# A token and channel mixer behind attention: the first channel product of the last two chunks in seven block products instead of eight

## The chip, the cores and the metric

The kernel runs on one core of a Trainium2 chip. The metric is the device time of one execution in microseconds (us). Five engines work side by side: TensorE (PE in the profile; PEld are its weight loads), VectorE (DVE), ScalarE (ACT), GpSimd (POOL) and SyncE (SP), which here issues the DMAs.

## The reference

Attention over 4 batches, 8 heads, 768 positions and head size 64, with a mask (8 global keys, a window of 96) and a linear bias; then a token mix and a channel mix, each of two products with a relu between. The mixes read the attention's output as `x` of 768 x 512 for each batch.

```python
def _moe_ref(x, w_tok1, w_tok2, w_ch1, w_ch2):
    xt = x.transpose(0, 2, 1)
    h = np.maximum(xt @ w_tok1, 0.0) @ w_tok2          # 768 -> 256 -> 768, over positions
    u = x + h.transpose(0, 2, 1)
    h2 = np.maximum(u @ w_ch1, 0.0) @ w_ch2            # 512 -> 1536 -> 512, over channels
    return (u + h2).astype(np.float32)
```

All is float32. The weights arrive as 64-bit words and are decoded on the chip.

## The kernel before

TensorE multiplies here in a float32 form that keeps fewer bits (F32R). Each operand is therefore split in a high part and a low part (`uh`, `ul` for u; `hh`, `hl` for the hidden layer; two halves of a `wc` tile for a channel weight), and each product is made of three matmuls: high by high, high by low, low by high. ScalarE makes the high part (copy or relu), VectorE or GpSimd subtracts it to get the low part.

The stages, all in one program:

- *Weights* (`weights`): 30 pieces of 128 x 512. ScalarE and VectorE decode them (two steps each), ScalarE makes the high part, VectorE or GpSimd the low. Pieces 0 to 5 are the token weights `w1h`, `w1l`, `w2h`, `w2l`; the rest the channel weights, `A[f]` (first product) and `Z[f]` (second), f from 0 to 11.
- *Attention* (`pair`): 48 steps, 12 to a batch, each of two heads and 256 queries: scores `sp`, maximum, exponent, sum, norm, transposes (by TensorE as `tp`, or from step 20 on by a DMA, `p<-r`), values `op`, and the output is put in `x`. Scores and values use TensorE in quarters of 64 x 64; everything else uses it whole.
- *Token mix* (`tokens`): per batch, six transposes `xtp`, first product `pj`, relu, and last product `pu` in tiles of 256 and 512 positions; VectorE adds `pu` to `x`, then `uh` and `ul` are made.
- *Channel mix* (`channel`): the 4 x 768 positions are cut into 6 chunks of 512 (`q`), so a chunk can span two batches. For each f, `first` makes a bank `hp` by 12 matmuls (4 slices of channels by 3), ScalarE takes its relu `hh`, VectorE the low part `hl`, and `second` adds 12 matmuls to four banks `acc` that are kept over all 12 f. At the end GpSimd makes `o` = uh + ul, VectorE adds `acc`, and SyncE stores it.

The order on every engine is written down ahead of time by `Plan.record`: each piece of work has a cost, a rank, what it must follow, and tokens that it takes and gives back (tile buffers by name, eight PSUM banks). The planner walks through its own clock and lets each engine take the ready piece of lowest rank; `TURN` is a price on changing between the two forms of TensorE. The ranks come from the tables at the end (`WEIGHTS`, `LOADS`, `CHANNEL`, `PAIRS`, `PRI`, `MIXES`). Each engine then runs its list strictly in order, so a wait holds up all that stands behind it. Because all operations pass through one helper, the profile shows line 235 for nearly all of them; the names of tiles tell them apart.

Of the kernel before, what the change touches and what calls it, by code (L numbers as in the profile page):

```python
# [9 lines left out]
F32 = mybir.dt.float32  # L10
# [58 lines left out]
def f32(ap):  # L69
    return ap.bitcast(F32)  # L70
# [173 lines left out]
class Fast:  # L244
# [157 lines left out]
    def pair(self, v):  # L402
# [132 lines left out]
        if v:  # L535
# [1 line left out]
                [f"load{v}"], r - PRI['q'])  # L537
        wp = ["w"] if wide else ["p", "p"]

        add(f"S{v}", "pe", 0.68 if j else 0.58, scores, ([f"q{v}"] if v else []) + ([f"ul{b - 1}{4 * len(spans(b - 1)) - 1}"] if b > 1 else []), r,  # L540
            [("sp", v, 0), ("sp", v, 1)], ["hl"] if FIRST <= v < PER else [], "quarters")
        for e in range(2):
            add(f"max{v}{e}", "dve", 0.58 if j else 0.52, lambda e=e: maxima(e), [f"S{v}"] + ([f"max{v}0"] if e else []),
# [27 lines left out]
    def tokens(self, b):  # L571
# [58 lines left out]

        def high_u(i):
            c, q, s, w, o = place(i)
            if o == 0:
                self.u[q, c] = [self.us.tile([P, W], F32R, tag=f"u{q % 2}", name=n) for n in ("uh", "ul")]
            act.copy(out=self.u[q, c][0][:, o:o + w], in_=self.x[b, c][:, s:s + w])

# [18 lines left out]
        for i in range(4 * len(segs)):  # L655
            c, q, s, w, o = place(i)
            k = r[NS + i]
            end = i // 4 == len(segs) - 1
            add(f"U{b}{i}", "pe", 6 * (w / 2400 + 0.013), lambda i=i: up(i),
                [f"jl{b}0", f"jl{b}1", "low3", "low4", "low5"] + ([f"U{b}{i - 1}"] if i else []), k, [("pu", b, i)],  # L660
                [tag] * 4 if i == 4 * len(segs) - 1 else [])
            add(f"ua{b}{i}", "dve", 0.12 + w / 900, lambda i=i: sum_(i), [f"U{b}{i}"], k - PRI['mix'], (), [("pu", b, i)])
            add(f"uh{b}{i}", "act", 0.1 + w / 1000, lambda i=i: high_u(i), [f"ua{b}{i}"], k - PRI['mix'], [f"u{q % 2}"] * 2 if o == 0 else [])
            add(f"ul{b}{i}", dict(pool=0.1 + w / 410, dve=0.12 + w / 900), 0, lambda en, i=i: low_u(i, en), [f"uh{b}{i}"],
                k - PRI['mix'], (), (["x"] if b else ["w"]) if end else [])


    def channel(self, q):

        add, dve, act, pool = self.plan.add, self.dve, self.act, self.pool  # L670
        last = CHUNKS * NF - 1
        hid, g = {}, {}

        def first(k):
            f = k % NF
            g["hp"] = ps = self.bank("hp", k)
            n = 0
            for c in range(4):
                for w, x in ((0, 0), (0, 1), (1, 0)):
                    self.pe.matmul(out=ps, lhsT=self.A[f][w][:, P * c:P * c + P], rhs=self.u[q, c][x],  # L680
                                   start=n == 0, stop=n == 11)
                    n += 1
            hid[k] = [ps, None, None]

        def high(k):
            hid[k][1:] = [self.hl.tile([P, W], F32R, tag="hl", name=n) for n in ("hh", "hl")]
            act.activation(out=hid[k][1], in_=hid[k][0], func=AF.Relu)

        def low(k):
            ps, hh, hl = hid[k]  # L690
# [11 lines left out]
        final = q == CHUNKS - 1  # L702

        def base(c):
            uh, ul = self.u[q, c]
            o = self.xs.tile([P, S], F32, tag="x", name="o")[:, :W] if final else self.io.tile([P, W], F32, tag="io", name="o")
# [12 lines left out]
        for f in range(NF):  # L719
            k = q * NF + f  # L720
            r = rank("channel", k)
            add(f"F{k}", "pe", 2.73, lambda k=k: first(k), ready + [f"low{6 + 2 * f}"] + ([f"F{k - 1}"] if k else []),
                r - PRI["F"], [("hp", k)])
            add(f"fh{k}", "act", 0.63, lambda k=k: high(k), [f"F{k}"], r - PRI['hid'], ["hl", "hl"])
            add(f"fl{k}", "dve", 0.7, lambda k=k: low(k), [f"fh{k}"], r - PRI["hid"], (), [("hp", k)])
            for i, cs in enumerate(((0,), (1,), (2,), (3,)) if k == last else ((0, 1), (2, 3))):
                add(f"G{k}{i}", "pe", 0.68 * len(cs), lambda k=k, cs=cs: second(k, cs),
                    [f"fl{k}", f"low{7 + 2 * f}"] + ([f"G{k}{i - 1}"] if i else [f"G{k - 1}1"] if k else []), r,
                    [("acc", q, c) for c in cs] if f == 0 else [], ["hl", "hl"] if cs[-1] == 3 else [])
        for c in range(4):  # L730
            add(f"base{q}{c}", "pool", 1.42, lambda c=c: base(c), [f"F{k}"], r, ["x" if final else "t"], [tag] * 2)
            add(f"out{q}{c}", "dve", 0.68, lambda c=c: total(c), [f"G{k}{c if k == last else c // 2}", f"base{q}{c}"], r - 30,
                [], [("acc", q, c)])
            pieces = parts(q)
            for i, cut in enumerate(pieces):
                add(f"store{q}{c}{i}", "sp", 0.7, lambda c=c, cut=cut: store(c, *cut), [f"out{q}{c}"], r - 30, (),
                    ["x" if final else "t"] if i == len(pieces) - 1 else [])

    def run(self):
        self.setup()  # L740
# [16 lines left out]

TURN = 96.75  # L760

BUSY = dict(dve=2.1, act=0.8, pool=1.6, sp=0.0)

# [284 lines left out]
```

## Time and profile before

| | us |
|---|---|
| median of 3 runs (lowest, highest) | 599.16 (597.72, 599.68) |
| the profiled execution | 596.46 |
| its span, first to last instruction | 595.1 |
| TensorE busy in it | 573.7 |
| VectorE, ScalarE, GpSimd busy | 307.4, 261.8, 208.5 |

The profile is of one execution. Its time is the span and 1.36 us around it. A busy time counts an engine as busy from an instruction's start to its end; matmuls overlap, so the distance from one start to the next tells more than the mean length of one. The granted TensorE clock was 0.997 of full speed over the span.

### The profile page before, as it was taken

Reading aid. Unit: us, or ns where it says so; the run is one execution under the profiler, and the core shown is the slowest. Engines: PE = TensorE matmul, PEld = TensorE weight load, DVE = VectorE, ACT = ScalarE, POOL = GpSimd, SP = SyncE. Lnnn points to the kernel's source line nnn. Section 1 sums busy time; section 2 is a strip of 40 time slices with the busy share of each in tenths; the row PEclk is TensorE's granted clock in tenths of the full one; section 3 lists DMA queues with packets and bytes.
Section 4 is the critical chain, followed back from the end, with each engine's and each line's share of the span. In section 5 each row is a group of like instructions: output and inputs, shape, how many; then the busy total and the mean of one; then the engine's idle time right before and its main releaser. Section 6 shows DMA issues by size and latency. Waiting matters only on the chain.

```text
span 595.1 us, 11893 instructions
## 1 busy us (share of the span) xinstructions
PE 573.7 (96%) x4456; PEld 465.4 (78%) x4456; DVE 307.4 (52%) x890; ACT 261.8 (44%) x713; POOL 208.5 (35%) x352
## 2 busy tenths in 40 slices
PE   4999999999999999999999999999999999999994
PEld 2878778778888878876888887677888888888883
DVE  5999999989433654574341147656526101121112
ACT  5999988987213443444330135646423101101010
POOL 4888787644212432443023026333504200040000
PEclk9999999999999999999999999999999999999998
DMA  7983378792001556386100015784201000020002
GB/s 266 342 350 117 116 253 306 198 257 91 0 2 70 140 133 150 77 169 160 50 1 1 0 72 116 183 172 127 54 1 66 6 0 1 0 72 0 1 0 77
DMA packets 62289, 62.46 MB, mean 105 GB/s; under 512 B 46864, under 2 KB 50064, under 8 KB 62224
## 3 DMA queue, kind: packets, MB, share of 16 engines
q1 hardware_dynamic: 62080, 61.62, 35.6%
q8 instruction: 37, 0.61, 0.4%
q14 instruction: 28, 0.23, 0.1%
q10 hardware_dynamic: 144, 0.00, 0.0%
HBM read 44.30 MB, written 6.29 MB: 85 GB/s over the span
## 4 chain that ended last, share of the span: by engine, by line
PE 82%; DMA 7%; DVE 4%; POOL 2%; issue 2%; SPq 1%; ACT 1%; POOLq 0%; DVEq 0%; ACTq 0%
PE acc L235 30%; PE hp L235 30%; PE pu L235 6%; PE pj L235 5%; PE op L235 5%; PE sp L235 4%; DMA e<-pk 3%; DMA p<-r 3%; PE tp L235 2%; PE xtp L235 1%; DVE pp L235 1%; DMA out<-o 1%; POOL pp L235 1%; POOL p L235 1%; DMA w<-wc 1%
## 5 line engine op out<-in xcount | busy, mean ns | idle before, releaser
L235 PE MATMUL hp<-uh,wc 128*128 128x512 f32 x576 | 185.3, 391 | 0.0
L235 PE MATMUL acc<-hh,wc 128*128 128x512 f32 x576 | 181.9, 397 | 0.0
L235 ACT ACTIVATE hh<-hp 128x512 fp32r<-128x512 f32 x72 | 42.9, 596 | 200.6 <-PE hp L235 198.6
L235 DVE SCALAR_TENSOR_TENSOR hl<-hp,hh 128x512 fp32r<-128x512 f32 x72 | 49.5, 687 | 155.1 <-ACT hh L235 155.0
L235 PEld LDWEIGHTS hp<-uh,wc 128*128 128x128 f32 x576 | 108.1, 188 | 23.4 <-issue 0.6
L235 PEld LDWEIGHTS acc<-hh,wc 128*128 128x128 f32 x576 | 105.2, 188 | 24.7 <-issue 3.3
L235 PE MATMUL acc<-hl,wc 128*128 128x512 f32 x288 | 112.7, 391 | 1.2 <-DVE hl L235 1.2
L235 PE MATMUL hp<-ul,wc 128*128 128x512 f32 x288 | 112.1, 389 | 0.0
L235 POOL TENSOR_SCALAR p<-p,st 128x192 f32<-128x192 f32 (+1 forms) x132 | 73.4, 574 | 34.1 <-DVE st L235 16.7
L235 DVE COPY r<-p 128x768 uint16<-128x768 uint16 x81 | 55.6, 694 | 43.7 <-POOL p L235 23.4
L235 PEld LDWEIGHTS acc<-hl,wc 128*128 128x128 f32 x288 | 54.1, 188 | 14.1 <-DVE hl L235 2.5
L235 PEld LDWEIGHTS hp<-ul,wc 128*128 128x128 f32 x288 | 54.1, 188 | 11.0
L235 ACT ACTIVATE p<-p,st 128x192 f32<-128x192 f32 (+1 forms) x132 | 57.4, 437 | 11.3 <-DVE st L235 11.1
L235 POOL TENSOR_TENSOR ul<-x,uh 128x512 fp32r<-128x512 f32 (+1 forms) x18 | 20.7, 1153 | 99.6 <-ACT uh L235 99.2
L235 POOL TENSOR_TENSOR o<-uh,ul 128x512 f32<-128x512 f32 x24 | 31.7, 1348 | 66.0 <-DMA out<-o 63.7
L235 POOL TENSOR_SCALAR e<-e,sc 128x256 f32<-128x256 f32 x37 | 21.6, 586 | 93.2 <-DMA e<-pk 82.8
L235 DVE SCALAR_TENSOR_TENSOR t<-w,t 128x512 int32<-128x512 int32 x60 | 47.2, 800 | 1.4 <-ACT w L235 0.9
L235 ACT COPY r<-p 128x768 uint16<-128x768 uint16 x31 | 32.9, 1067 | 32.8 <-DMA p<-r 30.9
L235 PE MATMUL sp<-e 64*64 64x192 f32 (+1 forms) x624 | 33.7, 332 | 10.1 <-ACT e L235 5.9
L235 DVE CUSTOM_DVE_ANT_0 p<-sp,bias 128x192 f32<-128x192 f32 (+1 forms) x132 | 37.7, 342 | 8.9 <-PE sp L235 8.8
L235 PEld LDWEIGHTS sp<-e 64*64 64x64 f32 x624 | 22.4, 139 | 15.7 <-ACT e L235 6.6
L235 PEld LDWEIGHTS op<-r,e 64*64 64x64 f32 x832 | 23.2, 133 | 10.5 <-issue 6.8
(90 smaller groups left out, 710.6 us busy)
## 6 DMA issues: line engine op xcount, KB each, us to landing
e<-pk SPq DMA_DIRECT2D x24, 592.0 KB, 4.0
w<-wc SPq DMA_DIRECT2D x24, 512.0 KB, 6.4
e<-pk SPq DMA_DIRECT2D x14, 560.0 KB, 5.3
out<-o SPq DMA_DIRECT2D x16, 256.0 KB, 2.1
unit<-pk SPq DMA_DIRECT2D x9, 384.0 KB, 5.4
w<-w SPq DMA_DIRECT2D x6, 512.0 KB, 7.4
out<-o SPq DMA_DIRECT2D x16, 128.0 KB, 1.9
keys<-pk SPq DMA_DIRECT2D x8, 208.0 KB, 5.2
```

What stands on the lines that cost most here:

```text
L235: ins = getattr(self.engine, name)(*args, **kw)
```

## The change

For the last two chunks (numbers 4 and 5) together, the first channel product is seen as a 2 x 2 block product: the channels in two halves, the pieces f and f + 6 as the two rows of weights, and the two chunks as the two columns of data. Strassen's scheme (in Winograd's form) needs seven block products for it where the plain one has eight. A *quad* is one f from 0 to 5; it gives four hidden tiles, called 11, 21 (chunk 4, pieces f and f + 6), 12, 22 (chunk 5).

- The data sums T1 to T4 are made once, behind the last batch's token mix: VectorE subtracts, ScalarE makes the high parts, VectorE the low parts (`td`, `th`, `tl`). They lie in the token weights' tiles and in attention buffers that are free by then.
- The weight sums S1, S2 are made for each quad a quad ahead, by GpSimd or VectorE (`sa`, `sb`), with high parts on ScalarE (`sh`) and low parts by VectorE or GpSimd (`sl`).
- The products `P` run in the order 1, 5, 2, 7, 6, 3, 4, six matmuls each, into four banks; 2, 3 and 4 add onto the bank of 1, 5 and 7.
- The sums of products are made by VectorE (`plus`), after a copy of product 1 by ScalarE (`keep`). Relu and low part follow as before, for chunk 5 into tiles that stay.
- The second product of chunk 4 (`G`) runs between the products; that of chunk 5 (`H`) comes last, one column of 128 channels after the other, 36 matmuls each. The last tile is added and stored in two halves.
- u of chunk 5 is split for two of its four channel slices only, and in the last batch by VectorE alone.
- The scores of batches 2 and 3 wait for the mix's last product instead of the last low part of u; and the planner's tables and `TURN` are new.

```diff
-        add(f"S{v}", "pe", 0.68 if j else 0.58, scores, ([f"q{v}"] if v else []) + ([f"ul{b - 1}{4 * len(spans(b - 1)) - 1}"] if b > 1 else []), r,
+        add(f"S{v}", "pe", 0.68 if j else 0.58, scores, ([f"q{v}"] if v else []) + ([f"U{b - 1}{4 * len(spans(b - 1)) - 1}"] if b > 1 else []), r,
...
+            if q == CHUNKS - 1 and c < 2:
+                continue
...
+        def product(f, x):
+            q = W // 2
+            a, b = self.A[f], self.A[f + M]
+            lhs = {1: [t[:, :q] for t in a], 2: [t[:, q:] for t in a], 4: [t[:, q:] for t in b]}
...
+            for d in range(2):
+                xs = {1: lambda: self.u[qa, d], 2: lambda: self.u[qa, d + 2], 3: lambda: self.u[qb, d + 2], 4: lambda: g["T", 4, d],
+                      5: lambda: g["T", 1, d], 6: lambda: g["T", 2, d], 7: lambda: g["T", 3, d]}[x]()
+                for w, r in ((0, 0), (0, 1), (1, 0)):
+                    pe.matmul(out=ps, lhsT=ws[w][:, P * d:P * d + P], rhs=xs[r], start=first and n == 0, stop=n == 5,
+                              skip_group_check=True)
+                    n += 1
+        def keep(f):
+            g["u2", f] = self.io.tile([P, W], F32, tag="io", name="u2")
+            act.copy(out=g["u2", f], in_=g["ps", f, 1])
+        def plus(f, out, ps, other):
+            if (out, f) not in g:
+                g[out, f] = self.mix.tile([P, W], F32, tag="p", name=out)
+            dve.tensor_tensor(out=g[out, f], in0=g["ps", f, ps], in1=g[other, f], op=ALU.add)
...
+        for f in range(M):
+            add(f"sa{f}", dict(dve=1.36, pool=2.84), 0, lambda e, f=f: whole(f, e),
+                [f"low{6 + 2 * f}", f"low{6 + 2 * (f + M)}", f"V{last_v - 1}"] + ([f"sb{f - 1}"] if f else []) + (["tl40", "tl41"] if f > 1 else []), s)
+            add(f"sb{f}", dict(dve=1.6, pool=3.2), 0, lambda e, f=f: mixed(f, e), [f"sa{f}", f"V{last_v}"] + ([f"sl{f - 1}0", f"sl{f - 1}1"] if f else []), s)
...
+            add(f"keep{f}", "act", 0.6, lambda f=f: keep(f), [f"P{f}1"], v, ["t"])
+            add(f"u2{f}", "dve", 0.68, lambda f=f: plus(f, "u2", 2, "u2"), [f"P{f}6", f"keep{f}"], v, (), [("hp", f, 2)])
+            add(f"u4{f}", "dve", 0.68, lambda f=f: plus(f, "u4", 3, "u2"), [f"P{f}5", f"u2{f}"], v, ["mix"])
+            add(f"u7{f}", "dve", 0.68, lambda f=f: plus(f, "u4", 4, "u4"), [f"P{f}7", f"u4{f}"], v)
+            add(f"c12{f}", "dve", 0.68, lambda f=f: plus(f, "c12", 3, "u2"), [f"P{f}3", f"u2{f}"], v, ["mix"], [("hp", f, 3)])
+            add(f"c21{f}", "dve", 0.68, lambda f=f: plus(f, "u2", 4, "u2"), [f"P{f}4", f"c12{f}"], v, (), [("hp", f, 4)])
...
+                if (q, c) == (qb, 3):
+                    b, s, w, o = pieces[0]
+                    pieces = [(b, s + i * w // 2, w // 2, o + i * w // 2) for i in range(2)]
...
-        for q in range(CHUNKS):
+        for q in range(CHUNKS - 2):
             self.channel(q)
+        self.last()
...
-TURN = 96.75
+TURN = 241.81
...
-PAIRS = [(103.53, 7.38), (232.79, 7.58), (299.85, 14.06)]
+PAIRS = [(119.72, 6.24), (217.78, 12.78), (353.61, 5.31)]
```

Three places of the planned order follow. On TensorE before, the end of a first product (`hp`) of chunks 4 and 5 and the start of the second product (`acc`) of the f before:

```order
L235 MATMUL hp<-uh,wc 128x512 x2
L235 MATMUL hp<-ul,wc 128x512
L235 MATMUL hp<-uh,wc 128x512
L235 MATMUL acc<-hh,wc 128x512 [waits Activation_49]
L235 MATMUL acc<-hh,wc 128x512
```

And with the change, products 1 (`uh`, `ul` by `wc`) and 5 (T1, which lies in `w2h` and `w2l`, by S1 in `w1h`) of a quad, ahead of the second product on the sum c21 of the quad before:

```order
L235 MATMUL hp<-uh,wc 128x512
L235 MATMUL hp<-ul,wc 128x512
L235 MATMUL hp<-uh,wc 128x512 x2
L235 MATMUL hp<-ul,wc 128x512
L235 MATMUL hp<-uh,wc 128x512
L235 MATMUL hp<-w2h,w1h 128x512 [waits Activation_49]
L235 MATMUL hp<-w2l,w1h 128x512
L235 MATMUL hp<-w2h,w1h 128x512
L235 MATMUL hp<-w2l,w1h 128x512 x3
L235 MATMUL acc<-hh,wc 128x512 [waits Activation_49]
L235 MATMUL acc<-hh,wc 128x512
L235 MATMUL acc<-hl,wc 128x512 [waits DVE_49]
```

Where 12 matmuls made one hidden tile, 12 make two products, and the second product behind them waits for ScalarE and VectorE's work on the product 4 that stands just ahead of these rows.

On VectorE before, the end of the program: the last batch's mix, then 12 low parts and 4 totals for each of the two chunks:

```order
L235 TENSOR_TENSOR x<-pu,x 128x512 x4
L235 TENSOR_TENSOR o<-acc,o 128x512 x4
L235 SCALAR_TENSOR_TENSOR hl<-hp,hh 128x512 x12
L235 TENSOR_TENSOR o<-acc,o 128x512 x4
```

With the change, one quad (`u_5641` is the running sum of product 1 and others, `u_5682` that for tile 22, `c_5709` is c12; `e_61` holds S1 and S2 in full):

```order
L235 SCALAR_TENSOR_TENSOR hl<-hp,hh 128x512 [waits Activation_49]
L235 TENSOR_TENSOR w1h<-e_61,w1h 128x512 [waits PE_49,Activation_49]
L235 TENSOR_TENSOR u_5641<-hp,u_5641 128x512 [waits DMAHW2_49,DVE_49,PE_49]
L235 TENSOR_TENSOR u_5682<-hp,u_5641 128x512 [waits DVE_49]
L235 TENSOR_TENSOR u_5682<-hp,u_5682 128x512 [waits DVE_49]
L235 SCALAR_TENSOR_TENSOR hid<-u_5682,hid 128x512 [waits DMAHW4_49,Activation_49]
L235 TENSOR_TENSOR c_5709<-hp,u_5641 128x512 [waits PE_49]
L235 TENSOR_TENSOR w1l<-e_61,w1h 128x512 [waits Activation_49]
L235 TENSOR_TENSOR u_5641<-hp,u_5641 128x512 [waits DVE_49,PE_49]
L235 SCALAR_TENSOR_TENSOR hid<-c_5709,hid 128x512 [waits Activation_49]
L235 SCALAR_TENSOR_TENSOR hl<-u_5641,hh 128x512 [waits Activation_49]
```

Two low parts for two f have become five sums, four low parts and two low parts of weight sums, and the low part of a weight sum (`w1l`) stands between c12 and c21.

On ScalarE before, behind the last batch's mix, the copies of u's high part and then nothing but relus:

```order
L235 ACTIVATE hh<-hp 128x512 [waits PE_49]
L235 CAST uh<-x 128x256 [waits DVE_49] x4
L235 CAST uh<-x 128x512 [waits DVE_49,Pool_49] x3
L235 CAST uh<-x 128x512 [waits Pool_49]
L235 ACTIVATE hh<-hp 128x512 [waits PE_49,Activation_49]
```

With the change, the same place ends in the first quad's copy of product 1 (`u_5641<-hp`):

```order
L235 ACTIVATE hh<-hp 128x512 [waits PE_49,Activation_49]
L235 CAST uh<-x 128x512 [waits Pool_49] x2
L235 CAST t_5615<-rough 128x512 [waits DVE_49,Pool_49]
L235 COPY u_5641<-hp 128x512 [waits DVE_49,DMAHW2_49,PE_49,Activation_49]
L235 ACTIVATE hh<-hp 128x512 [waits PE_49,Activation_49]
```

That copy waits for a DMA too (`DMAHW2`): the store of chunk 3's second tile, whose buffer it takes.

## Rows read from the trace of the kernel before

**Rows 1.** The page: busy time of each engine, share of the span, instructions.

```profile
PE 573.7 (96%) x4456; PEld 465.4 (78%) x4456; DVE 307.4 (52%) x890; ACT 261.8 (44%) x713; POOL 208.5 (35%) x352
```

**Rows 2.** Windows: length; busy TensorE, its loads, VectorE, ScalarE, GpSimd; clock; DMA; GB/s.

```profile
0.00:20.00 20.00, 11.64 (x138) 8.32 (x142) 12.45 (x71) 13.18 (x50) 9.60 (x44) 1.00 0.86 298
20.00:60.00 40.00, 38.76 (x680) 31.82 (x676) 39.02 (x159) 39.26 (x136) 34.47 (x75) 1.00 0.69 255
60.00:100.00 40.00, 38.16 (x409) 31.17 (x410) 37.21 (x97) 35.14 (x94) 30.00 (x36) 1.00 0.64 226
100.00:150.00 50.00, 49.96 (x377) 39.84 (x376) 44.04 (x92) 42.27 (x90) 27.02 (x30) 1.00 0.61 179
...
200.00:300.00 100.00, 98.50 (x868) 78.92 (x868) 53.34 (x165) 43.36 (x122) 31.45 (x60) 1.00 0.53 124
300.00:450.00 150.00, 149.26 (x1139) 120.59 (x1138) 72.48 (x219) 57.41 (x161) 45.94 (x77) 1.00 0.31 72
450.00:595.00 145.00, 137.44 (x607) 113.52 (x605) 27.70 (x41) 16.74 (x28) 16.50 (x13) 0.99 0.07 23
```

**Rows 3.** Chain of waits, last 200 us: start, length, engine and line, count.

```profile
413.90 1.59 PE acc L235 x6
...
431.31 1.38 PE acc L235 x6
...
445.83 8.34 PE pu L235 x48
...
576.57 5.44 PE hp L235 x24
582.01 3.41 PE acc L235 x15
```

**Rows 4.** Instructions by form, TensorE: operation, shapes, count | busy, mean ns | idle.

```profile
L235 PE MATMUL hp<-uh,wc 128*128 128x512 f32 x576 | 185.3, 391 | 0.0
...
L235 PEld LDWEIGHTS hp<-uh,wc 128*128 128x128 f32 x576 | 108.1, 188 | 23.4 <-issue 0.6 <-ACT x L235 0.3
```

**Rows 5.** Instructions by form, the other three engines (same columns).

```profile
L235 DVE SCALAR_TENSOR_TENSOR hl<-hp,hh 128x512 fp32r<-128x512 f32 x72 | 49.5, 687 | 155.1 <-ACT hh L235 155.0
L235 DVE SCALAR_TENSOR_TENSOR t<-w,t 128x512 int32<-128x512 int32 x60 | 47.2, 800 | 1.4 <-ACT w L235 0.9
L235 ACT ACTIVATE hh<-hp 128x512 fp32r<-128x512 f32 x72 | 42.9, 596 | 200.6 <-PE hp L235 198.6 <-PE acc L235 1.8
...
L235 POOL TENSOR_TENSOR wc<-t,wc 128x512 fp32r<-128x512 f32 x15 | 22.1, 1478 | 16.5 <-ACT wc L235 15.1 <-DMA w<-wc 1.3
...
L235 POOL TENSOR_TENSOR ul<-x,uh 128x512 fp32r<-128x512 f32 x12 | 15.6, 1300 | 59.1 <-ACT uh L235 58.7
...
L235 DVE TENSOR_TENSOR x<-pu,x 128x512 f32<-128x512 f32 x16 | 11.0, 690 | 6.9 <-PE pu L235 6.7
...
L235 DVE TENSOR_TENSOR wc<-t,wc 128x512 fp32r<-128x512 f32 x9 | 6.8, 759 | 1.1 <-ACT wc L235 1.1
L235 DVE TENSOR_TENSOR x<-pu,x 128x256 f32<-128x256 f32 x16 | 6.4, 419 | 5.4 <-PE pu L235 5.1
...
L235 POOL TENSOR_TENSOR ul<-x,uh 128x256 fp32r<-128x256 f32 x6 | 5.1, 860 | 40.5 <-ACT uh L235 40.5
```

**Rows 6.** Timeline of the end: start, length, engine, operation, idle before it.

```profile
585.51 2.73 DVE L235 TENSOR_TENSOR o<-acc,o 128x512 f32<-128x512 f32 x4 [2.15 <-PE acc L235]
...
586.23 3.61 SPq L235 DMA_DIRECT2D out<-o  x4
...
587.06 0.39 PE L235 MATMUL acc<-hl,wc 128*128 128x512 f32 x1
```

**Rows 7.** DMA issues on the page; the output tile; the closing semaphores.

```profile
out<-o SPq DMA_DIRECT2D x16, 128.0 KB, 1.9
...
DMA to landing us min/median/max: 1.7/2.0/6.7
...
L1044 SPq EVENT_SEMAPHORE  x8: 17/28/28, 592.8 to 595.1; - x8
```

More of the change, by code (lines that the diff above doesn't have):

```diff
@@ L632, in high_u @@
             c, q, s, w, o = place(i)
-            if o == 0:
+            if (q, c) not in self.u:
                 self.u[q, c] = [self.us.tile([P, W], F32R, tag=f"u{q % 2}", name=n) for n in ("uh", "ul")]
@@ L662, in tokens @@
             add(f"ua{b}{i}", "dve", 0.12 + w / 900, lambda i=i: sum_(i), [f"U{b}{i}"], k - PRI['mix'], (), [("pu", b, i)])
+            if q == CHUNKS - 1 and c < 2:
+                continue
             add(f"uh{b}{i}", "act", 0.1 + w / 1000, lambda i=i: high_u(i), [f"ua{b}{i}"], k - PRI['mix'], [f"u{q % 2}"] * 2 if o == 0 else [])
-            add(f"ul{b}{i}", dict(pool=0.1 + w / 410, dve=0.12 + w / 900), 0, lambda en, i=i: low_u(i, en), [f"uh{b}{i}"],
-                k - PRI['mix'], (), (["x"] if b else ["w"]) if end else [])
+            add(f"ul{b}{i}", dict(dve=0.12 + w / 900) if b == B - 1 else dict(pool=0.1 + w / 410, dve=0.12 + w / 900), 0, lambda en, i=i: low_u(i, en), [f"uh{b}{i}"],
+                k - PRI['mix'], (), ([] if b == B - 1 else ["x"] if b else ["w"]) if end else [])
     def channel(self, q):
         add, dve, act, pool = self.plan.add, self.dve, self.act, self.pool
-        last = CHUNKS * NF - 1
         hid, g = {}, {}
@@ L700, in second @@
                                    start=f == 0 and i == 0, stop=f == NF - 1 and i == 2)
-        final = q == CHUNKS - 1
         def base(c):
             uh, ul = self.u[q, c]
-            o = self.xs.tile([P, S], F32, tag="x", name="o")[:, :W] if final else self.io.tile([P, W], F32, tag="io", name="o")
+            o = self.io.tile([P, W], F32, tag="io", name="o")
             g["o", c] = o
@@ L723, in channel @@
                 r - PRI["F"], [("hp", k)])
[L724 to L728, printed above, removed]
+            add(f"fh_{k}", "act", 0.63, lambda k=k: high(k), [f"F{k}"], r - PRI['hid'], ["hl", "hl"])
+            add(f"fl_{k}", "dve", 0.7, lambda k=k: low(k), [f"fh_{k}"], r - PRI["hid"], (), [("hp", k)])
+            for i, cs in enumerate(((0, 1), (2, 3))):
+                add(f"g{k}_{i}", "pe", 0.68 * len(cs), lambda k=k, cs=cs: second(k, cs),
+                    [f"fl_{k}", f"low{7 + 2 * f}"] + ([f"g{k}_{i - 1}"] if i else [f"g{k - 1}_1"] if k else []), r,
                     [("acc", q, c) for c in cs] if f == 0 else [], ["hl", "hl"] if cs[-1] == 3 else [])
         for c in range(4):
-            add(f"base{q}{c}", "pool", 1.42, lambda c=c: base(c), [f"F{k}"], r, ["x" if final else "t"], [tag] * 2)
-            add(f"out{q}{c}", "dve", 0.68, lambda c=c: total(c), [f"G{k}{c if k == last else c // 2}", f"base{q}{c}"], r - 30,
+            add(f"base{q}{c}", "pool", 1.42, lambda c=c: base(c), [f"F{k}"], r, ["t"], [tag] * 2)
+            add(f"out{q}{c}", "dve", 0.68, lambda c=c: total(c), [f"g{k}_{c // 2}", f"base{q}{c}"], r - 30,
                 [], [("acc", q, c)])
@@ L788, in rank @@
         return CHANNEL[0] + CHANNEL[1] * at[0]
-WEIGHTS = [71.26, 9.54, 24.38, 24.05]
-LOADS = [13.15, 6.65, 38.51, 3.54]
-CHANNEL = [162.7, 6.43]
-PAIRS = [(103.53, 7.38), (232.79, 7.58), (299.85, 14.06)]
-PRI = {'q': -1.3, 'max': 19.6, 'exp': 3.4, 'sum': 46.9, 'norm': -2.6, 'T': -2.6, 'back': 11.2, 'split': -78.6, 'join': -1.1, 'V': 47.2, 'put': 16.0, 'F': 5.5, 'mix': 1.2, 'hid': 28.8, 'high': 15.9}
-MIXES = [-31.47, 214.66, 304.69]
+WEIGHTS = [82.59, 11.43, 0.91, 26.98]
+LOADS = [10.58, 4.16, 407.44, 1.08]
+CHANNEL = [176.2, 6.52]
+PAIRS = [(119.72, 6.24), (217.78, 12.78), (353.61, 5.31)]
+PRI = {'q': -16.6, 'max': 27.3, 'exp': -7.0, 'sum': 90.7, 'norm': -19.4, 'T': -22.4, 'back': 52.4, 'split': -95.1, 'join': 5.2, 'V': 13.2, 'put': 25.2, 'F': 7.0, 'mix': -9.7, 'hid': 49.7, 'high': 21.0}
+PRI2 = {'early': 159.0, 'quad': 34.3, 'mixed': 108.7, 'second': -69.0, 'step': -14.4, 'tail': -66.4}
+MIXES = [154.62, 92.38, 36.73]
 @with_exitstack
```

175 lines of the change are left out of this document (174 added, 1 removed).

## The prediction

> **What bounds the kernel now.** I read the engines' busy times first, then the same by stage, then the chain of waits of the last 200 us, then single operations and the tail. TensorE is busy 573.7 of 595.1 us, every other engine half of it or less [rows 1]. By stage, TensorE lacks 8.36 us in the first 20, then 1.24, 1.84, 0.04, 1.50 and 0.74 in the stages shown from 20 to 450 us, 5.36 together; VectorE and ScalarE are as full as TensorE only up to 100 us (39.02 and 39.26 of 40 us between 20 and 60). From 450 us on it lacks 7.56 us, all behind the last matmul, which starts at 587.06 and runs 0.39 [rows 2, 6]. In the chain the end is nothing but first and second products back to back: 24 matmuls in 5.44 us, so 226.7 ns each [rows 3]. Their weight loads take 188 ns, less than that, and stay beneath them [rows 4]. So a 128x512 matmul taken out between 150 us and the end is worth 226.7 ns, as long as its successors never wait.
>
> **The change, part by part.**
>
> *Products removed.* Two chunks with 12 pieces each of 12 matmuls are 288 for the first product. Now six quads of seven products of six matmuls do it: 252. The order of TensorE agrees, 36 rows fewer, all else equal in count. 36 x 0.2267 = -8.16 us. I found no row of a product accumulated over six matmuls in a bank of its own with sums over several banks behind it, but the mix's last product is six matmuls to a bank: 48 of them, half 256 wide, take 8.34 us without a gap [rows 3]. So a six-matmul group pays no entry price: 0 extra; the other end is the price of a change of form, 0.21 us for each of 42 products, 8.8 us.
>
> *Sums added, VectorE and ScalarE.* A quad adds on VectorE five sums of PSUM (0.69 each, as the mix's sum), four lows (0.69) and two lows of the weight sums (0.76): 7.7 us; on ScalarE a copy, four relus and two copies, 7 x 0.60 = 4.2 us [rows 5]. A quad is 42 + 24 = 66 matmuls, 14.96 us, and lies in a stage in which both engines are nearly idle (27.70 and 16.74 us of 145) [rows 2]. Totals fit twice over, so only chains can cost. The tightest is the second product of the sum c21. Count from the end E of product 4: product 3 ended at E-1.36; VectorE makes c12, then the weight low queued behind it (until E+0.19), then c21 (E+0.88), low 12 (E+1.57), low 21, whose relu was ready at E+1.58 (E+2.36). TensorE has products 1 and 5 of the next quad first (12 matmuls, 2.72 us) and two matmuls on the high part, so it asks at E+3.17: 0.8 us to spare. Product 5 needs the bank that c12 empties, at E-0.57, and asks at E+1.36. The low behind product 2 (0.60 + 0.69 + 0.1) is hidden by products 7 and 6 (2.72). Cost 0. If all cover were gone: 1.4 + 2.4 us, some 3.8 per quad, 23 us.
>
> *The sums before the first quad.* After the mix's last product TensorE has 66 matmuls of the chunks before (14.96 us; the kernel before has 12). VectorE then has 19 instructions up to the last low of the sums T, 19 x 0.69 = 13.1 us [rows 5], and of these only the first six stand before product 5, which comes at 16.3 us. Cost 0. One wait is new in kind: ScalarE's copy of product 1 takes a buffer that the second store of chunk 3 must have left. Its last product ends at 13.6 us, two totals 0.69 each make 15.1, the store lands 2.0 us later [rows 7], the copy needs 0.60: 17.8, and product 2, which must not write before, would start at 17.7. With the relu behind it in ScalarE's queue I put +0.3 us; with landings of 1.7 and 6.7 us [rows 7] it is 0 and +4.8. The DMA is quiet there (share 0.07) [rows 2], so the median counts.
>
> *Weight sums on GpSimd.* Two of 512 (1.30) and four of 256 (0.86) per quad: 6.0 of 14.96 us [rows 5], a quad ahead: 0 by themselves. But a rule speaks against them. The low of a channel weight, with both inputs in SBUF, took VectorE 0.759 us; the low of the hidden layer, with one in PSUM, 0.687; GpSimd's weight lows took 1.478 where its token lows took 1.300 [rows 5]. So a meeting costs VectorE under 0.1 us on the mean: three such lows in the tight chain give 0.2 of the 0.8 us to spare, and nothing in the sum. The Trainium skill (SBUF — State Buffer, section Who interferes with whom) says that a VectorE instruction with two SBUF inputs contends with a GpSimd one that reads SBUF, and that the loser fully blocks for the whole instruction; the trace shows lengthening, not whole blocks. That mechanism is the slower rival below.
>
> *The tail.* Before: four totals, one behind each quarter of the last product, four stores of 256 KB crowded together; the fourth is issued at about 588.3 and SyncE sees it landed at 592.8 [rows 6, 7], 5.35 us after the last matmul's end at 587.45. Now the four columns are finished one after another, 36 matmuls (8.16 us) apart, so only the last tile is late, in two halves: two totals of 256 (0.42 each, 0.1 to start) [rows 5], then a 128 KB store, 1.9 us [rows 7]: 2.9 us. -2.45 us; ends 0 (the last store as slow as now) and -2.6.
>
> *The attention's order.* The scores' wait now ends with the mix's last product, the price of a form change rises to 241.81 and all ranks are new. In TensorE's order the runs of one form fall by four, two returns from quarter form to full: six matmuls after such a return take 1.59 us, elsewhere 1.38 [rows 3], so about 0.23 each way with the entry, -0.5 us together. For the waits, the first and second products that stand between a batch's first scores and its transposes rise from 192 to 252 (batch 1), 330 to 432 (batch 2), 228 to 258 (batch 3): each wait has more behind it. At best all 5.36 us of idle go; at worst as much comes on top (an estimate: no row bounds it). I take -1.0.
>
> Sum: -8.16 - 2.45 - 0.5 - 1.0 + 0.3 = -11.8. The profiled execution took 596.46, span 595.1 plus 1.36: it would take 584.7. The median of the runs shown is 2.7 us above it; the same step from 599.16 gives 587.4.
>
> **Rivals.**
> 1. *The order costs instead of paying.* For: batch 1's mix now comes after 2.5 more weight pairs, five pieces of two 0.80 us steps each, 8.0 us of VectorE [rows 5] in a stage where it has 8.75 of 90 us free [rows 2]. Against: the 60 extra products give TensorE 13.6 us of work meanwhile. Idle doubles: 587.4 + 1.0 + 5.4 = 593.8.
> 2. *GpSimd holds VectorE up, and it gets slower.* Place: in each quad the next weight sums on GpSimd start right when the weight low is done, beside c21, low 12 and low 21. If each of three two-input lows waited for a whole GpSimd sum of 1.30, that is 3.9, less 0.8 to spare, 3.1 us on six quads: 18.6, giving 606. It decides from a hold-up of 0.8 + 11.8/6 = 2.8 us per quad. Against: 0.759 beside 0.687. A mild form, one block of 1.30 in each quad, costs 0.5 x 6 = 3 us: 590.4.
> 3. *The change doesn't do what it says:* 42 short products pay 0.21 us each to enter, and 8.8 of the gain is lost: 596.2. Against: the gapless 48 of the mix.
>
> **How the numbers follow.** Forecast 0.66 (its own range 584 to 590); rival 1 0.14; the mild form of 2 0.09; 2 in full 0.05; 3 0.06. About 0.3%, 1.8 us, is what a measurement of this kernel can tell from no change, so faster means under 597.4. The first three cases are faster, 0.89; rival 3 mostly too, half of it within the bound: faster 0.92, same 0.03, slower 0.05. Low end: idle halves (-2.7 for -1.0), no new wait, a shorter tail still: 583. High end: rival 1, 593.8. Left out are most of 2 in full and of 3, and a little below.
>
> **What would show it.** 5.44 us per 24 matmuls in the last 130 us without idle before acc or hp, and matmuls of the two chunks' first product at 252: step 1. The time from the last matmul's end to SyncE's first closing semaphore near 2.9 us: the tail. TensorE's idle between 20 and 450 us under 5.4: the order. A gap before the first quad's second product shows the buffer. Wrong it is if TensorE waits on VectorE in every quad, or if VectorE's two-input lows grow beyond 0.9 us.

## The result and the profile after

| | before | after |
|---|---|---|
| median of the compared runs, us | 598.60 (597.72 to 599.68, 4 runs) | 591.41 (590.07 to 593.89, 4 runs) |
| ratio, 95% interval | | 0.9884 [0.9842, 0.9926] |
| profiled execution, us | 596.46 | 593.89 |
| its span | 595.1 | 592.0 |
| last matmul's end | 587.45 | 585.14 |

The change saves 7.2 us by the medians, where 11.8 were forecast. The two profiled executions are only 2.6 us apart: that of before lies 2.1 us under its median, that of after 2.5 above its own. What the traces show must therefore be split by stage and compared over more than one execution.

The page's first part, as in [rows 1]: TensorE has 36 matmuls and 6.7 us of work less, VectorE 49.5 us more.

```profile
PE 567.0 (96%) x4420; PEld 460.4 (78%) x4420; DVE 356.9 (60%) x952; ACT 276.2 (47%) x743; POOL 234.4 (40%) x377
```

Windows of after, for [rows 2] (same columns; the last one begins 3 us behind the mix's end):

```profile
20.00:60.00 40.00, 36.69 (x649) 30.53 (x642) 38.67 (x156) 37.88 (x133) 35.19 (x75) 1.00 0.65 241
...
100.00:150.00 50.00, 47.45 (x321) 37.36 (x320) 44.97 (x85) 40.92 (x84) 30.04 (x29) 0.97 0.62 183
...
200.00:300.00 100.00, 100.00 (x793) 81.12 (x792) 49.93 (x153) 36.54 (x107) 28.89 (x52) 1.00 0.48 113
300.00:450.00 150.00, 148.47 (x1197) 119.50 (x1196) 84.22 (x231) 64.80 (x180) 57.80 (x91) 1.00 0.36 80
450.00:592.00 142.00, 134.91 (x594) 111.01 (x592) 66.08 (x95) 29.59 (x49) 26.39 (x25) 0.99 0.07 23
```

TensorE lacks 3.31 us between 20 and 60 (1.24 before) and 2.55 between 100 and 150 (0.04 before, and there at a granted clock of 0.97); between 200 and 300 it lacks nothing more (1.50 before). From 20 to 450 us it lacks 9.3 us in all, where the forecast wanted under 5.4. So the order moved idle time to the front, where the forecast had it shrink.

The largest new wait, in the timeline of after (start, length, engine, operation; in brackets the idle time before and what ended it):

```profile
127.75 5.17 DVE L235 SCALAR_TENSOR_TENSOR t<-w,t 128x512 int32<-128x512 int32 x5 [0.51 <-issue]
...
131.50 1.19 PE L235 MATMUL sp<-e 64*64 64x192 f32 x18
...
134.05 0.68 DVE L235 SCALAR_TENSOR_TENSOR hl<-hp,hh 128x512 fp32r<-128x512 f32 x1
...
134.78 1.55 PE L235 MATMUL sp<-e 64*64 64x192 f32 x14 [2.10 <-DVE hl L235]
```

Scores wait 2.1 us for the bank that a low part of the hidden layer empties. That low part stands on VectorE behind five steps of weight decoding and more; the waits of before show none between 100 and 150 us. Behind the wait the granted clock is near the lower of its two levels for 3.3 us (columns as in [rows 2]):

```profile
134.70:138.00 3.30, 3.22 (x19) 2.19 (x20) 3.27 (x10) 2.29 (x6) 1.87 (x2) 0.53 0.00 0
```

So the wait costs more than its 2.1 us, by some 1.5 us (an estimate: 3.3 us at about half speed).

The chain of waits at the end, for [rows 3]:

```profile
450.83 1.70 DVE rough L235
...
453.74 1.71 DVE w1l L235
...
455.47 1.29 DVE rough L235 x2
456.76 0.61 DVE hl L235
...
457.42 5.28 PE acc L235 x22
462.70 6.84 PE hp L235 x30
469.54 2.72 PE acc L235 x12
472.26 5.44 PE hp L235 x24
...
549.78 35.37 PE acc L235 x156
...
585.18 0.08 DVE x L235
```

From 457.4 on it is products back to back: 24 first products in 5.44 us, as in [rows 3], and 156 second products in 35.37, 226.7 ns each. Ahead of that, VectorE's queue of sums is the chain, up to a low part that waits for its turn there and that a second product of the cover needs; two of the steps (a sum and a low part) have 1.70 and 1.71 us in it, where their neighbours have 0.6. The timeline of after shows what they met there, and the same for low 21 in a quad:

```profile
450.31 1.68 POOL L235 TENSOR_TENSOR o<-uh,ul 128x512 f32<-128x512 f32 x1 [6.95 <-DVE t L235]
450.75 1.78 DVE L235 TENSOR_TENSOR rough<-x,rough 128x512 f32<-128x512 f32 x1
...
490.05 1.89 POOL L235 TENSOR_TENSOR e<-e,e 128x256 f32<-128x256 f32 x2 [4.12 <-DVE w1l L235]
491.37 1.12 DVE L235 SCALAR_TENSOR_TENSOR hl<-u,hh 128x512 fp32r<-128x512 f32 x1
```

GpSimd ends at 451.99 and 491.94, VectorE 0.54 and 0.55 us later, at 452.53 and 492.49: here a VectorE instruction of 0.69 with two inputs in SBUF hardly moves until GpSimd's has ended.

### The profile page after: what moved, and what is told of

Same layout as the page of the kernel before. It is cut to its first block, busy times and chain, and to the rows that moved or that the text cites. A ratio compares the mean times of both kernels' runs of the same rounds, so it can differ in the third digit from the quotient of the medians.

```text
span 592.0 us, 11933 instructions
## 1 busy us (share of the span) xinstructions
PE 567.0 (96%) x4420; PEld 460.4 (78%) x4420; DVE 356.9 (60%) x952; ACT 276.2 (47%) x743; POOL 234.4 (40%) x377
## 5 line engine op out<-in xcount | busy, mean ns | idle before, releaser
L235 PE MATMUL acc<-hh,wc 128*128 128x512 f32 x480 | 152.1, 398 | 0.0
L235 PE MATMUL hp<-uh,wc 128*128 128x512 f32 x432 | 144.8, 394 | 0.0
L235 PEld LDWEIGHTS acc<-hh,wc 128*128 128x128 f32 x480 | 88.2, 189 | 21.2 <-issue 2.8
L235 PEld LDWEIGHTS hp<-uh,wc 128*128 128x128 f32 x432 | 81.1, 188 | 18.4 <-ACT x L235 0.6
L235 PE MATMUL acc<-hl,wc 128*128 128x512 f32 x240 | 94.3, 393 | 0.2 <-DVE hl L235 0.2
L235 PE MATMUL hp<-ul,wc 128*128 128x512 f32 x216 | 84.3, 390 | 0.0
L235 ACT ACTIVATE hh<-hp 128x512 fp32r<-128x512 f32 x54 | 32.1, 594 | 83.8 <-PE hp L235 82.0
L235 DVE SCALAR_TENSOR_TENSOR hl<-hp,hh 128x512 fp32r<-128x512 f32 x54 | 36.9, 683 | 52.2 <-ACT hh L235 52.0
L235 PEld LDWEIGHTS hp<-ul,wc 128*128 128x128 f32 x216 | 40.6, 188 | 7.9
L235 PE MATMUL acc<-hid,wc 128*128 128x512 f32 x144 | 33.0, 389 | 0.0
## 6 DMA issues: line engine op xcount, KB each, us to landing
e<-pk SPq DMA_DIRECT2D x24, 592.0 KB, 4.3
```

Of the source, the lines that this page charges most:

```text
L235: ins = getattr(self.engine, name)(*args, **kw)
```

## How the stages are compared

Orders put different numbers of first and second products into a stage. To compare it, take its length by the end of a batch's last mix product (`pu`; the start of the next matmul is taken for it), and subtract 0.2267 us for each first and second product that stands in it. What is left is attention, mixes and waits:

| run | to batch 1's mix | on to batch 2's | on to batch 3's | sum |
|---|---|---|---|---|
| before | 109.8 | 43.0 | 42.5 | 195.3 |
| after | 117.3 | 38.5 | 44.8 | 200.6 |

For before, batch 1's mix ends at 164.4 behind 241 products (the one that starts then counted in): 164.4 - 54.6 = 109.8; for after at 180.1 behind 277. The profiled executions of e1, e4 and e5 have after's order of the attention; their sums are 201.0, 197.1 and 200.4, so one execution is good for 2 us or so, and the mean of the four is 199.8. Part of that scatter goes with the clock: between 100 and 150 us it is 0.97 in after, e1, e3 and e6, which take 116.7 to 118.8 us to batch 1's mix, and 1.00 in e4 and e5, which take 115.3 and 115.6; the order up to there is the same in all six.

## Experiments

Ratios are to the kernel before on the same chip, with 95% intervals.

**e1: eight products.** Product 1 runs twice, so the first product has its 288 matmuls again.

```diff
-            for d in range(2):
+            for d in ((0, 1, 0, 1) if x == 1 else (0, 1)):
...
-                    pe.matmul(out=ps, ..., start=first and n == 0, stop=n == 5, ...)
+                    pe.matmul(out=ps, ..., start=first and n % 6 == 0, stop=n % 6 == 5, ...)
```

> The changed kernel with the six matmuls of product 1 made twice in each quad, the first time overwritten: 36 matmuls of 128x512 more, nothing else. Theory 1 (TensorE is the bound of the last stage and of the whole): each costs its 226.7 ns, 36 x 0.2267 = 8.16 us more than the changed kernel, 599.6 against 591.4, and the last matmul ends 8.2 us later. Theory 2 (the quads wait for VectorE's sums, so part of the removed matmuls were idle time anyway): less than 6 us more, since the longer product 1 hides waits.

Measured: 600.22 us, 1.0048 [1.0033, 1.0063]. From its chain:

```profile
473.98 6.80 PE hp L235 x30
480.78 2.72 PE acc L235 x12
...
558.30 35.37 PE acc L235 x156
```

30 matmuls where after has 24, at the same 226.7 ns. From the mix's end to the last matmul's end it takes 146.21 us, after 138.08: 8.13 for 36 matmuls, 8.16 forecast. Short groups of six pay no entry: rival 3 falls. The whole gain of the change is this term; without it the change is slower than before.

**e2: the old tables** (`TURN`, `WEIGHTS`, `LOADS`, `CHANNEL`, `PAIRS`, `PRI`, `MIXES`) in the changed kernel.

```diff
-TURN = 241.81
+TURN = 96.75
...
-PAIRS = [(119.72, 6.24), (217.78, 12.78), (353.61, 5.31)]
+PAIRS = [(103.53, 7.38), (232.79, 7.58), (299.85, 14.06)]
```

> The changed kernel with the price of a form change and all ranks of the kernel before (the five new ranks of the quads stay). Theory 1 (the prediction: the new order is worth 1.5 us): 1.5 us slower than the changed kernel, 593. Theory 2 (the new order costs: it delays batch 1's mix, and TensorE idles more up to 150 us): 4 to 6 us faster, 585.5 to 587.5, with batch 1's first transposes back at about 134 us.

Measured: 611.50 us, 1.0244 [1.0217, 1.0271]. What TensorE waits for behind 450 us (in total, times, longest), and then the chain there:

```profile
PE hp L235 <- ACT u L235: 8.3, 1, 8.3
PE hp L235 <- DVE u L235: 5.5, 5, 1.5
```

```profile
467.71 2.04 DMA out<-o
...
469.85 0.59 ACT u L235
...
470.48 5.15 PE hp L235 x12
475.63 2.74 PE acc L235 x12
```

Both theories had looked at the attention alone, and both are far off. Only 12 matmuls are left to cover VectorE's sums, as in the order before. Behind the mix TensorE loses some 20 us against after, 15 of them in waits, and the wait for the store's landing, which I had priced at 0.3 us, is really there: store, copy `u`, product 2. The 5.5 us are hardly a matter of the cover: in five of the six quads product 3 waits for the sum that empties its bank, so the old tables order the quads worse too. After 8.3 us of standstill twelve matmuls take 5.15 us instead of 2.72, half the speed, at a granted clock of 0.55, near the lower of its two levels:

```profile
470.40:475.60 5.20, 5.12 (x13) 4.07 (x14) 3.99 (x6) 1.97 (x5) 1.69 (x1) 0.55 0.04 17
```

But the attention is about as fast as before (196.8 in sum). So the new tables cost some 3 to 4 us in the attention and buy some 20 behind it.

**e3: the kernel before with the new tables**, its products and its scores' wait unchanged (the edit of e2 the other way round).

> The kernel before with the new price and ranks (its own products, tail and scores' wait). Theory 1: 1.5 us faster than before, 597.1. Theory 2: 4 to 6 us slower than before, 602.6 to 604.6, and the loss lies ahead of batch 1's mix.

Measured: 605.05 us, 1.0129 [1.0102, 1.0157]. By stage 116.7, 43.4 and 46.3: the loss up to batch 1's mix comes with the tables alone, and the gain in batch 2 (38.5 in after) is not from the tables alone. By the medians the tables cost the kernel before 7.7 us, somewhat more than theory 2's 4 to 6; this profiled execution is 3.1 us above its median.

**e4: the last tile whole.**

```diff
-                if (q, c) == (qb, 3):
+                if False:
```

> The changed kernel with its last tile added and stored whole. From the last matmul's end to SyncE's first closing semaphore the changed kernel took 4.34 us. Theory 1 (the landing of the last store ends it): one total of 0.69 and a store of 256 KB that lands after 2.0 to 2.9 us: about as long, 4.3 to 4.6. Theory 2 (SyncE's branch behind its last issue ends it, 2.7 us, and the landing lies beneath it): issue ends at 0.83 + 0.33 = 1.16, so 3.9 us, 0.4 less. In the time neither is more than 0.5 us.

Measured: 589.95 us, 0.9892 [0.9865, 0.9919], as after. From the last matmul's end to SyncE's first closing semaphore 4.09 us, after 4.34, before 5.40: the two halves gain nothing. That is between theory 2's 3.9 and theory 1's 4.3.

**e5: the weight sums on VectorE** instead of GpSimd, at the same places of the order.

```diff
-                add(f"sa{f}", ..., lambda e, f=f: whole(f, e), ...)
+                add(f"sa{f}", ..., lambda e, f=f: whole(f, dve), ...)
```

and `mixed(f, dve)` likewise.

> The changed kernel with the weight sums made by VectorE at the very places of the order where GpSimd made them (every other instruction stays). The sums of the next quad, 2 x 0.69 + 4 x 0.42 = 3.1 us, then stand in VectorE's queue just behind the weight low, ahead of c21 and its low. Theory 1 (the tight chain has 0.8 us to spare, as the prediction counted): TensorE waits 3.1 - 0.8 = 2.3 us in about five quads, 11 us more than the changed kernel, a ratio to before of 1.007; low 21 back at 0.69 us from a median of 1.09. Theory 2 (GpSimd's contention was what VectorE lost, and the chain has more to spare): the ratio stays at 0.988 within 0.003, or falls.

Measured: 595.09 us, 0.9962 [0.9939, 0.9984]. Neither theory's number came. VectorE's low 21 by form (busy, mean ns | idle) behind 470 us, first in after, then in e5 (`hl<-u,hh`):

```profile
L235 DVE SCALAR_TENSOR_TENSOR hl<-u,hh 128x512 fp32r<-128x512 f32 x6 | 5.8, 968 | 0.4
```

```profile
L235 DVE SCALAR_TENSOR_TENSOR hl<-u,hh 128x512 fp32r<-128x512 f32 x6 | 4.1, 686 | 0.2
```

GpSimd does hold VectorE up: without it, low 21 falls from 968 to 686 ns. TensorE's waits behind 450 us, of after and of e5:

```profile
PE acc L235 <- DVE hl L235: 0.2, 1, 0.2
```

```profile
PE acc L235 <- DVE hl L235: 1.1, 4, 0.3
```

VectorE has 3.0 us more to do in a quad (two sums of 0.68, four of 0.42), but the expectation had their place wrong. The timeline of e5, from the sum c21 to the matmul that needs low 21, and then that matmul in after (where low 21 starts at 491.37 and takes 1.12, as shown above):

```profile
489.88 0.69 DVE L235 TENSOR_TENSOR u<-hp,u 128x512 f32<-128x512 f32 x1
490.49 0.75 DVE L235 TENSOR_TENSOR e<-e 128x256 f32<-128x256 f32 x2
491.15 0.88 DVE L235 TENSOR_TENSOR e<-e,e 128x256 f32<-128x256 f32 x2
491.95 0.68 DVE L235 SCALAR_TENSOR_TENSOR hid<-c,hid 128x512 fp32r<-128x512 f32 x1
492.55 0.68 DVE L235 SCALAR_TENSOR_TENSOR hl<-u,hh 128x512 fp32r<-128x512 f32 x1
493.16 1.28 DVE L235 TENSOR_TENSOR e<-wc 128x512 f32<-128x512 f32 x2
...
493.29 0.50 PE L235 MATMUL acc<-hl,wc 128*128 128x512 f32 x1 [0.28 <-DVE hl L235]
```

```profile
492.95 0.39 PE L235 MATMUL acc<-hl,wc 128*128 128x512 f32 x1
```

The two sums of 512 come behind low 21, where they delay nothing. Only the four of 256 stand ahead of it, 1.46 us, and TensorE has to wait for low 21 in four quads. In after low 21 ends 0.46 us ahead of its matmul in the four quads in which it meets GpSimd, and 0.89 ahead in the last two, in which it meets no sum. So the tight chain has 0.89 us to spare, close to the 0.8 that the prediction counted; GpSimd takes 0.43 of it, and that stays hidden. Of e5's loss against after, 1.8 us lie behind the mix (139.91 us to the last matmul's end, for 138.08); the rest is not settled.

**e6: the old wait of the scores** in batches 2 and 3, with the new tables.

```diff
-f"U{b - 1}{4 * len(spans(b - 1)) - 1}"
+f"ul{b - 1}{4 * len(spans(b - 1)) - 1}"
```

> The changed kernel with the scores' wait of before (for the last low part of u), all else as changed. The planner then leaves no first or second product of the chunks before between the last token mix and the first quad (540 matmuls behind the mix instead of 606). Theory 1 (the 66 matmuls are what hides the sums T): 15 to 20 us slower than the changed kernel, with TensorE idle behind the mix as in the run with the old tables. Theory 2 (the scores' wait matters only for its own stage): within 3 us of the changed kernel.

Measured: 606.36 us, 1.0155 [1.0112, 1.0199]. By stage 117.4, 41.1 and 46.9: 2.7 and 2.0 us worse than after in batches 2 and 3. So a part of the gain in batch 2 hangs on the scores' wait. It is not that alone either: e2 has the new wait with the old tables and takes 43.8 there, as long as before. Tables and wait gain only together. Behind the mix it loses some 6 us more: the mix now ends behind all 1152 products of the first four chunks, and nothing covers the sums. That is less than e2 pays with 12 matmuls of cover; e2 has the wait for the store and those inside the quads besides. By the ratios e6 is some 16 us slower than after, as theory 1 had it; the two profiled executions are 11 us apart, and only these are accounted for here.

**e7 and e8: which numbers cost the front.** e7 gives batch 1 its old ranks; e8 these and the old ranks of weights and loads.

```diff
-WEIGHTS = [82.59, 11.43, 0.91, 26.98]
-LOADS = [10.58, 4.16, 407.44, 1.08]
+WEIGHTS = [71.26, 9.54, 24.38, 24.05]
+LOADS = [13.15, 6.65, 38.51, 3.54]
...
-PAIRS = [(119.72, 6.24), (217.78, 12.78), (353.61, 5.31)]
+PAIRS = [(103.53, 7.38), (217.78, 12.78), (353.61, 5.31)]
...
-MIXES = [154.62, 92.38, 36.73]
+MIXES = [-31.47, 92.38, 36.73]
```

(e7 has the line of `PAIRS` alone.)

> The changed kernel with the ranks of batch 1's attention as before (one pair of numbers); its mix then follows 252 instead of 276 first and second products, and the rest of the order from batch 2 on keeps its counts. Theory 1 (the 5.5 us that the changed kernel loses up to batch 1's mix come from the ranks of batch 1): 3 to 5 us faster, ratio 0.981 to 0.984. Theory 2 (they come from the weights' and loads' ranks): no change, 0.988.

> The changed kernel with the ranks of weights, loads, batch 1's attention and batch 1's mix as before; batches 2 and 3 and the quads keep theirs. Theory 1 and 2 alike: if the loss up to batch 1's mix lies in any of these ranks, 4 to 6 us faster than the changed kernel, ratio 0.979 to 0.982. Theory 3 (it lies in the price of a form change or in the offsets inside a pair): no change.

Measured: e7 590.59 us, 0.9876 [0.9842, 0.9909], by stage 117.0, 39.4, 44.7: as after. e8 587.77 us, 0.9837 [0.9801, 0.9873], by stage 112.9, 38.3, 43.8: 2.8 us less than after by the ratios, where 4 to 6 were expected, with intervals that overlap. Windows of e8:

```profile
20.00:60.00 40.00, 36.79 (x625) 30.25 (x617) 37.33 (x153) 38.75 (x135) 34.26 (x74) 1.00 0.70 261
...
100.00:150.00 50.00, 48.56 (x359) 38.90 (x358) 44.26 (x83) 40.49 (x81) 25.40 (x27) 1.00 0.61 183
```

Between 100 and 150 the idle time falls from 2.55 to 1.44 us and the granted clock is back at 1.00; between 20 and 60 nothing changes. So of the 7.6 us that the front loses some 4 go with these ranks; e12 below has the old ranks of weights and loads alone and takes 113.3, so it is these that count.

**e9, e10 and e11: the rest of the front.** e9 is after with the old offsets `PRI` in batches 0 and 1 and for the weights, e10 is e8 with them, e11 is after with the old `TURN`.

```diff
+        PRI = PRI_OLD if b < 2 else PRI_NEW
```

```diff
-TURN = 241.81
+TURN = 96.75
```

> The changed kernel with the offsets of the attention's steps (PRI) of the kernel before for batches 0 and 1 and for the weights; everything behind batch 1, TURN and the cover of 66 matmuls as changed. In the order batch 1's mix then stands behind 204 first and second products instead of 276. Theory A (the order of the first two batches costs the changed kernel some 4 us, and the offsets are what costs it): the end of batch 1's mix, less 0.2267 us for each first and second product ahead of it, falls from 117.3 us (180.1 at 277 in the changed kernel) to the 110 of the kernel before, and the ratio to before is near 0.981. Rival B (what costs is the late weights and loads, which stay): no gain, the ratio is 0.988 as with the changed kernel.

> The version with the old ranks of weights, loads and batch 1 (ratio 0.9837 to before) and, on top, the old offsets (PRI) for batches 0 and 1 and for the weights. Theory A (offsets cost, and add to the 2.8 us that the weights' and loads' ranks gave): two to three us less than that version, a ratio of 0.979 to 0.980, the end of batch 1's mix normalised by 0.2267 us per product near 110 us (113.0 there). Rival B (weights and loads were all of it): 0.9837 again, normalised end near 113.

> The changed kernel with one number back: TURN, the price of a change between TensorE's two forms, 96.75 as before instead of 241.81. In TensorE's order the runs of one form rise from 92 to 106, and batch 3's mix stands behind 1062 first and second products instead of 1086, so 90 matmuls cover the sums before the first quad instead of 66. Theory A (a run of quarter form costs about 0.46 us for its entry and the return, as the 0.21 us of rows 3 each way gives, and the price has no other effect): 14 runs more are 7 pairs, 7 x 0.46 = +3.2 us on the changed kernel, a ratio of 0.9935. Rival B (the higher price makes waits, because work of the other form is held back, and costs as much as it saves): no difference, 0.988, with less idle time of TensorE between 130 and 160 us than the 4.6 us of the changed kernel.

Measured: e9 592.27 us, 0.9920 [0.9894, 0.9946], normalised end of batch 1's mix 118.0; e10 586.79 us, 0.9846 [0.9807, 0.9885], 112.2. No gain in either: the offsets by themselves are not it. e11: 600.43 us, 1.0079 [1.0049, 1.0109], some 11.6 us slower than after by the ratios and 5.2 by the profiled executions, more than theory A's 3.2 us either way. By stage 119.4, 39.7 and 46.7, 2.1, 1.2 and 1.8 us worse than after, each no more than one execution can settle. The higher price is clearly a gain as a whole, and more than 0.46 us for each pair of runs: it moves other work as well.

**e12: the very last store from ScalarE's queue**, on after with the old ranks of weights and loads.

```diff
-WEIGHTS = [82.59, 11.43, 0.91, 26.98]
-LOADS = [10.58, 4.16, 407.44, 1.08]
+WEIGHTS = [71.26, 9.54, 24.38, 24.05]
+LOADS = [13.15, 6.65, 38.51, 3.54]
...
-            self.sp.dma_start(...)
+            (self.act if (q, c) == (qb, 3) and o else self.sp).dma_start(...)
```

> The version with the old ranks of weights, loads and batch 1 (last matmul's end to SyncE's first closing semaphore 4.65 us there, SyncE's branch behind its last issue at 1.85, the last sum's end at about 0.8), with the very last store, the second half of the last tile, issued by ScalarE instead of SyncE, so that SyncE's last issue is the first half, at about 0.5. Everything else, TensorE's order too, is the same. Theory A (the closing follows SyncE's branch by 2.6 to 2.95 us and nothing else): the branch comes at about 0.9 and the first closing semaphore at 3.5 to 3.85. Rival B (the closing follows the landing of the last store by 0.9 to 1.2 us, and a store lands 2.0 us behind its issue): ScalarE issues at about 0.85, the store lands at 2.9 or a little later, and the closing comes at 3.9 to 4.2. Rival C (ScalarE's own branch takes the place of SyncE's): 4.2 to 4.6, as long as now. In the time, all are within 1.2 us: the ratio of that version, 0.9837, or 0.982 at best.

The expectation calls this e8 with the store moved. It is not quite: the ranks of batch 1's attention and mix are the new ones, and TensorE's order in the attention differs from e8's. The tail is the same, and the front shows what weights and loads do alone: 113.3 us to batch 1's mix, with no idle TensorE between 100 and 150 us but 5.2 us of it between 20 and 60.

Measured: 589.27 us, 0.9865 [0.9830, 0.9900], an interval that overlaps that of e8. SyncE's branch (second start), the stores, their landing and SyncE's closing semaphores (first and last start), in after and then in e12 (last matmul's end 581.66):

```profile
L1221 SPq COMPARE_BRANCH  x2: 46/48/49, 6.2 to 586.7; - x2
...
L235 SPq DMA_DIRECT2D out<-x x5: 332/333/638, 561.4 to 586.1; - x5
...
DMA to landing us min/median/max: 2.0/2.0/2.2
...
L1280 SPq EVENT_SEMAPHORE  x8: 17/28/28, 589.5 to 592.0; - x8
```

```profile
L1221 SPq COMPARE_BRANCH  x2: 46/48/49, 6.6 to 582.5; - x2
...
L235 ACTq DMA_DIRECT2D out<-x x1: 357/357/357, 582.5 to 582.5; - x1
...
DMA to landing us min/median/max: 2.0/2.1/2.5
...
L1280 SPq EVENT_SEMAPHORE  x8: 17/28/28, 585.3 to 587.8; - x8
```

Theory A holds: the branch comes 0.87 us behind the last matmul's end (1.60 in after), the closing 3.68 behind it (4.34). The last store lands at 582.5 + 2.5, only some 0.35 us ahead of the closing, where rival B wanted 0.9 to 1.2. Over all runs the first closing semaphore stands 2.5 to 3.0 us behind SyncE's branch. That the total does not follow has a second cause: from the first to the last closing semaphore it takes 2.5 us in e12, 1.1 in e8 and 1.1 to 3.1 over all runs; the runs don't say why.

## Why the prediction was right, and where not

The time lies in the range and on the side forecast, 4.0 us above the likeliest value. By its steps, in the profiled executions:

| term | forecast | shown | by |
|---|---|---|---|
| 36 products | -8.16 | -8.1 | e1 |
| sums in the quads | 0 | 0 | waits of after, e5 |
| sums before the first quad | 0 | +0.5 | chain of after, e2 |
| store under the copy | +0.3 | 0 | after; there in e2 |
| order (changes of form and waits) | -1.5 | +5.3 (+4.5 over four runs) | stages, e2, e3, e8 |
| tail | -2.45 | -1.06 | e4, e12 |

The terms shown make -3.4, the spans differ by 3.1; the closing semaphores of after stretch 0.2 us longer. By the medians the change saves 7.2 us, and the terms other than the order make -8.7: that leaves the order +1.5 us (-0.8 to +4.3 by the interval of the ratio). The execution of e4, which is close to its median, has +1.8 by its stages. So the order cost 1.5 to 5 us instead of gaining 1.5, and how much of that is common to most executions is open.

- *Products.* Right in mechanism and size.
- *Sums in the quads.* The cost of nothing holds, and the chain is as I counted it: 0.89 us to spare where it meets no GpSimd sum, for 0.8 (under e5). My price for GpSimd was wrong. From means [rows 5] I read that a meeting with GpSimd costs VectorE under 0.1 us, and weighed this against the Trainium skill (SBUF — State Buffer, section Who interferes with whom), which calls the ports that the two engines share an exclusive lock. The trace of after agrees with that rule: VectorE ends 0.54 to 0.55 us behind GpSimd's end, whatever is left of the latter, in the two long steps ahead of the first quad and in low 21 (968 ns on the mean). A mean over instructions most of which meet nothing hides that. Rival 2's mechanism is thus there; its price is not, because low 21 meets only the last 0.5 us of a short sum, which costs 0.43 us of the 0.89 to spare. So the sign of failure that I named, lows beyond 0.9 us, came without a failure in the quads. That the sums beside the lows are the short ones, and the wide ones come when the chain is done, I had not looked up: there the forecast was lucky.
- *Sums before the first quad.* I asked when product 5 needs its low part; what was late is a second product of the cover, whose own `hl` stands behind the sums in VectorE's queue; a gap of 0.4 us, some 0.5 in all. The two meetings with GpSimd put 2.2 us into that queue (1.70 and 1.71 for 0.6 each), more than the gap: it is the one place where rival 2's mechanism was paid for. The cover of 66 matmuls is just enough, and e2 shows what 54 fewer cost, with the old tables' waits in the quads on top.
- *Order.* The step that failed. I took the new ranks to remove all of the idle time at best and to double it at worst, and chose a small gain without a row for it. In fact, in the profiled executions, they lose 7.6 us up to batch 1's mix, gain 4.6 in batch 2, where tables and scores' wait work only together (e2, e3, e6), and lose 2.3 in batch 3. It is rival 1's place, and its cause in part: VectorE's weight steps come in front of what TensorE waits for, the clock falls behind that wait, and 4 us of the loss go with the ranks of weights and loads (e8, e12). What costs the other 3 us, 2 of them between 20 and 60 us, stays open: batch 1's ranks (e7), the offsets (e9, e10) and `TURN` (e11) are not it by themselves; all old tables together do bring it back (108.9 in e2). `CHANNEL`, the ranks of later batches and `TURN` together with the old ranks were not tried.
- *Tail.* I let the end follow the last store's landing. It follows SyncE's branch behind its last issue; the issue of before took longer (the branch 2.45 us behind the last matmul's end, the closing 5.40), and two halves mean one more issue. So -1.06 instead of -2.45.

The version with the change and the old ranks of weights, loads and batch 1 (e8) is the fastest found: 587.77 us, 0.9837 [0.9801, 0.9873], and with the old offsets (e10) 586.79, 0.9846. Its interval overlaps that of the changed kernel; the stage up to batch 1's mix (112.2 to 113.3 in e8, e10 and e12, 115.3 to 118.8 in the six profiled executions with the new front's order) does not.

## What to carry to other kernels

Count products taken out at their rate, and then ask what covers the work that stands in for them: here the cover had to be bought by another order, and the order gave a part of the gain back (1.5 us by the medians, 4.5 in the traces) at a place where nothing had been changed. Price a new order stage by stage, with the matmuls that it moved taken off, not by the idle time that it could save, and over more than one execution. And read the end of a program from the engine that closes it, not from the last store.

## What the hardware showed unexpectedly

- The closing semaphores come 2.5 to 3.0 us behind SyncE's branch, also when another queue issues the last store (e12); splitting the last store adds an issue and gains nothing (e4).
- After 8.3 us without work, twelve matmuls took 429 ns each instead of 227, at a granted clock of 0.55, then again 228 (e2). The granted clock also fell, to 0.53 for 3.3 us, behind a wait of 2.1 us (after).
- Beside a GpSimd sum of two SBUF inputs, a VectorE instruction of 0.69 us with two SBUF inputs took what was left of that sum and 0.55 us more: 1.12 in a quad, 1.78 ahead of the first.
